# Four more transposes moved from TensorE to the DMA queue, and five instead of two put ahead of the loads of v

## The chip, the cores and the metric

One core of a Trainium2 chip. The time is the device time of one execution in microseconds (us); medians are over several executions.

## The reference

A block of 2048 rows of 512 numbers: a layer norm; attention over 8 dilated positions (32 heads of 16, the positions 0, 2, ... 14 rows back); a gated GELU network of width 1792 on the same normalized rows; the two multiplied and added to the input.

```python
xn = _layernorm(x, axis=-1)
s = _A_ref(xn, A_wqkv, A_wo)      # q, k, v = xn @ wqkv; softmax over 8 dilated positions; @ wo
g = _silu(_B_ref(xn, B_w_gate, B_w_up, B_w_down))   # (gelu(xn@w_gate) * (xn@w_up)) @ w_down
return x + s * g
```

## The kernel before

The rows are worked on in four chunks of 512 rows (`j`), each of four tiles of 128 (`t`). A chunk goes through the gated projections (`glu`, 14 pairs), the q, k, v projections of the *next* chunk (`qkv`), four down projections (`down`), and after the first of these through `sums`: the softmax's denominators, the sums over v, and the logits of the next chunk.

Projections read the normalized rows transposed (`xnT`). Tiles are transposed in one of two ways:

```python
    def to_psum(t, cs=range(NC)):                # on TensorE, into PSUM; ScalarE copies it out
        ...
            nc.tensor.transpose(
                trs[t][:, c * P : (c + 1) * P], xns[t][:, c * P : (c + 1) * P], ident[:]
            )

    def transpose_by_dma(t, cs=range(NC)):       # by the DMA, four of 128x128 a tile
        ...
        for c in cs:
            nc.sync.dma_start(
                out=xnT[j][:, c, i * P : (i + 1) * P],
                in_=xns[t][:, c * P : (c + 1) * P],
                transpose=True,
            )
```

In chunk 1, tiles 4 and 5 go over TensorE and tiles 6 and 7 over the DMA. All DMAs are issued from one queue, in program order. v takes a way through DRAM: `copy_out` stores it (`vT<-vst`), and `load_v` reads it back in four loads, shifted by the dilated positions (`v_arr<-vT`). In the stretch of interest the order is:

```python
    at(("glu", 0, 0), transpose_by_dma, TPQ + 2, (0, 1))     # tile 6, two of four
    at(("glu", 0, 0), load_v, 0)
    at(("glu", 0, 0), transpose_by_dma, TPQ + 2, (2, 3))
    at(("glu", 0, 0), transpose_by_dma, TPQ + 3)             # tile 7
    at(("glu", 0, 0), load_late_weights)                     # w_down, wo
```

VectorE takes from there: eight products with v (`pv`, line 409), then sixteen products of q and k for chunk 1 (`pk`, line 337), which TensorE sums to the logits:

```python
    def sums(j):
        if j + 1 < NJ:
            nc.scalar.preload_act_table(AF.Exp)
        denominators(j)
        av_sums(j)
        if j + 1 < NJ:
            logits(j + 1)
        reciprocals(j)
        ...
```

The softmax here doesn't subtract the row's maximum and nothing guards it: scores larger than these inputs give would overflow.

## Time and profile before

| | kernel before |
|---|---|
| median of the first three runs | 228.55 us (228.47 to 228.56) |
| TensorE busy | 98% of the span |
| VectorE, ScalarE busy | 67%, 58% |
| first load of v issued, fourth landed | 26.11, 40.20 us |
| first product with v starts | 40.33 us |
| first gated projection to first output projection | 52.62 us |

The last row is the measure for what happens in the stretch concerned: from the start of the first `g_ps` matmul to that of the first `s_ps` matmul, read from the trace. The profile of the kernel before is of an execution of 228.39 us. The lines of the profile are in the prediction.

To read them: the span is the time from the first to the last instruction; the chain is the work that ended last, followed back step by step to what released it. PE is TensorE (PEld its weight loads), DVE is VectorE, ACT is ScalarE, POOL is GpSimd, SPq is the sequencer that issues the DMAs, and L311 is line 311 of the kernel. "x4" counts instructions, and a bracket gives the idle time before one and what ended it.

### The profile page before, as it was taken

To read this page: it belongs to the slowest core of one execution; us is meant where nothing else is said; L and a number is where in the kernel's file an instruction comes from. 1 tells how busy PE (TensorE), PEld (TensorE's weight loads), DVE (VectorE), ACT (ScalarE), POOL (GpSimd) and SP (SyncE) were. 2 spreads that over 40 slices of the span, in tenths; PEclk is the share of its full clock that TensorE was granted. 3 is DMA by queue.
4 is the path that set the end of the run, shared out by engine and by line. 5 is a ranking of instruction groups with operands and counts; after the bars stand their busy time and mean duration, and the time that the engine had idled before them with its cause. 6 is when DMAs were issued, how large, how long until landed. Compare 5 with 4: busy or idle time off the path is not lost.

```text
span 226.7 us, 3599 instructions
## 1 busy us (share of the span) xinstructions
PE 221.7 (98%) x1324; PEld 107.0 (47%) x1324; DVE 152.4 (67%) x280; ACT 132.1 (58%) x209; POOL 20.1 (9%) x67
## 2 busy tenths in 40 slices
PE   7999999999999999999999999999999999999993
PEld 4885444444444444444444444444444444444453
DVE  4689971999995489969813859925934448971434
ACT  4488679767631767676752466676763356756210
POOL 1026941000030000320000000000000000000000
PEclk9999999999999999999999999999999999999999
DMA  6999399942049921100219931100208940001002
GB/s 192 375 397 382 82 215 166 315 115 94 7 101 198 184 58 25 23 4 0 93 41 212 184 105 29 25 2 0 92 21 163 199 121 0 0 0 33 0 25 69
DMA packets 30130, 24.64 MB, mean 109 GB/s; under 512 B 10784, under 2 KB 29600, under 8 KB 30112
## 3 DMA queue, kind: packets, MB, share of 16 engines
q1 hardware_dynamic: 30112, 24.41, 45.0%
q8 instruction: 10, 0.16, 0.3%
q14 instruction: 8, 0.07, 0.1%
HBM read 18.74 MB, written 4.34 MB: 102 GB/s over the span
## 4 chain that ended last, share of the span: by engine, by line
PE 96%; DVE 1%; DMA 1%; issue 0%; ACT 0%; DVEq 0%
PE y_ps L460 21%; PE g_ps L266 21%; PE u_ps L266 21%; PE qkv_ps L266 16%; PE s_ps L476 6%; PE L_ps L355 3%; PE o_ps L423 3%; PE qk_ps L578 2%; DMA x_sb<-in_A_x_dram 1%; PE v_ps L578 1%; PE tr L224 1%; DVE stats L187 1%; PE den_ps L375 0%; DVE m L484 0%; DVE mv L190 0%
## 5 line engine op out<-in xcount | busy, mean ns | idle before, releaser
L266 PE MATMUL g_ps<-xnT,wg_sb 128*128 128x512 bf16 x224 | 57.5, 379 | 0.0
L266 PE MATMUL u_ps<-xnT,wu_sb 128*128 128x512 bf16 x224 | 57.5, 379 | 0.0
L460 PE MATMUL y_ps<-wd_sb,h 128*128 128x512 bf16 (+1 forms) x238 | 49.9, 367 | 0.0
L450 ACT ACTIVATE u<-u_ps 128x512 bf16<-128x512 f32 x56 | 33.5, 598 | 16.9 <-PE u_ps L266 16.9
L452 DVE TENSOR_TENSOR h<-ge,u 128x512 bf16<-128x512 bf16 x56 | 23.8, 424 | 29.0 <-ACT u L450 27.3
L448 ACT ACTIVATE ge<-g_ps 128x512 bf16<-128x512 f32 x56 | 33.5, 598 | 16.4 <-PE g_ps L266 16.3
L337 DVE TENSOR_TENSOR pk<-q_sb,k_sb 128x1024 bf16<-128x1024 bf16 (+1 forms) x56 | 38.9, 759 | 4.6 <-ACT k_sb L290 4.6
L409 DVE TENSOR_TENSOR pv<-E,v_arr 128x1024 bf16<-128x1024 bf16 (+1 forms) x48 | 39.7, 862 | 0.0
L266 PE MATMUL qkv_ps<-xnT,wqkv_sb 128*128 128x512 bf16 (+1 forms) x192 | 37.0, 352 | 0.0
L460 PEld LDWEIGHTS <-h 128*128 128x128 bf16 x238 | 23.0, 98 | 25.9 <-issue 1.3
L266 PEld LDWEIGHTS <-wu_sb 128*128 128x128 bf16 x224 | 21.9, 98 | 26.4
L266 PEld LDWEIGHTS <-wg_sb 128*128 128x128 bf16 x224 | 21.7, 98 | 26.3 <-issue 0.8
L468 ACT ACTIVATE sl<-y_ps 128x512 bf16<-128x512 f32 (+1 forms) x17 | 9.7, 572 | 32.6 <-PE y_ps L460 32.6
L266 PEld LDWEIGHTS <-wqkv_sb 128*128 128x128 bf16 x192 | 18.8, 98 | 17.6
L484 DVE TENSOR_TENSOR m<-s_ps,sl 128x512 bf16<-128x512 f32 (+1 forms) x17 | 11.1, 655 | 19.1 <-PE s_ps L476 19.1
L435 DVE TENSOR_TENSOR oT<-o_ps,rb 128x1024 bf16<-128x1024 f32 x8 | 9.4, 1219 | 11.7 <-DMA rb<-rs_d 11.7
L476 PE MATMUL s_ps<-wo_sb,oT 128*128 128x512 bf16 (+1 forms) x68 | 14.8, 366 | 0.0
L204 POOL TENSOR_TENSOR rstd<-rstd,mhalf 128x1 f32<-128x1 f32 x12 | 8.0, 670 | 71.1 <-DVE rstd L201 71.1
L290 ACT ACTIVATE vst<-qkv_ps 128x512 bf16<-128x512 f32 x14 | 8.4, 597 | 3.7 <-PE qkv_ps L266 3.7
L290 ACT ACTIVATE k_sb<-qkv_ps 128x512 bf16<-128x512 f32 x14 | 8.4, 602 | 3.2 <-PE qkv_ps L266 3.2
L290 ACT ACTIVATE q_sb<-qkv_ps 128x512 bf16<-128x512 f32 x14 | 8.3, 603 | 3.0 <-PE qkv_ps L266 3.0
L476 PEld LDWEIGHTS <-oT 128*128 128x128 bf16 x68 | 6.6, 98 | 7.2
(58 smaller groups left out, 126.6 us busy)
## 6 DMA issues: line engine op xcount, KB each, us to landing
v_arr<-vT SPq DMA_DIRECT2D x16, 520.0 KB, 8.4
vT<-vst SPq DMA_DIRECT2D x8, 256.0 KB, 2.3
out_dram<-o_t SPq DMA_DIRECT2D x15, 128.0 KB, 2.7
wg_sb<-in_B_w_gate_dram SPq DMA_DIRECT2D x2, 896.0 KB, 10.0
wu_sb<-in_B_w_up_dram SPq DMA_DIRECT2D x2, 896.0 KB, 10.7
wd_sb<-in_B_w_down_dram SPq DMA_DIRECT2D x1, 1792.0 KB, 10.8
wqkv_sb<-in_A_wqkv_dram SPq DMA_DIRECT2D x4, 384.0 KB, 4.6
x_sb<-in_A_x_dram SPq DMA_DIRECT2D x3, 512.0 KB, 10.3
```

The costliest lines, as they stand in the source:

```text
L266: nc.tensor.matmul(ps, lhsT=w[:, dk, lo : lo + P], rhs=xnT[j][:, dk, i0 : i0 + n], start=(dk == 0), stop=(dk == NC - 1),)
L290: nc.scalar.activation(out=dst, in_=ps, func=AF.Copy)
L337: nc.vector.tensor_tensor(out=st[j]["pk"][w][:, c0 : c0 + n, :], in0=st[j]["q"][:, c0 : c0 + n, :], in1=k_sb[j][:, c0 : c0 + n, off : off ...
L409: nc.vector.tensor_tensor(out=pv[:, d : d + n, :], in0=st[j]["E"][:, wh, :].unsqueeze(1).to_broadcast([P, n, TQ]), in1=st[j]["va"][:, 4 * ...
L435: nc.vector.tensor_tensor(out=oT[:, g : g + 2, :], in0=st[j]["o"][:, g : g + 2, :], in1=st[j]["rb"][:].unsqueeze(1).to_broadcast([P, 2, TQ ...
L448: nc.scalar.activation(out=ge[:], in_=g_ps[:], func=AF.Gelu_apprx_tanh)
L450: nc.scalar.activation(out=u[:], in_=u_ps[:], func=AF.Copy)
L452: nc.vector.tensor_tensor(out=h[:], in0=ge[:], in1=u[:], op=ALU.mult)
L460: nc.tensor.matmul(y[:], lhsT=st[j][fc][:, tt * P : (tt + 1) * P], rhs=wd_sb[:, fc, cols], start=(fc == 0), stop=(fc == NF - 1),)
L468: nc.scalar.activation(out=sl[:], in_=y[:], func=AF.Silu)
L476: nc.tensor.matmul(s[:], lhsT=st[j]["oT"][:, g, tt * P : (tt + 1) * P], rhs=wo_sb[:, g, cols], start=(g == 0), stop=(g == NC - 1),)
L484: nc.vector.tensor_tensor(out=m[:], in0=s[:], in1=sl[:], op=ALU.mult)
```

## The change

TensorE is the bound, so four transposes of tile 5 are taken from it. The queue stands idle for 3.8 us ahead of the loads of v, so three transposes are put into that hole: five stand ahead of the loads instead of two, seven behind instead of six.

```diff
     for i in range(TPQ):
         at(("down", 0, 1), moments, 2 * TPQ + i)
-        if i < 2:
-            at(("glu", 0, i), transpose, TPQ + i)
         at(("down", 0, 2), normalize, 2 * TPQ + i)
...
-    at(("glu", 0, 0), transpose_by_dma, TPQ + 2, (0, 1))
+    at(("glu", 0, 0), transpose, TPQ)
+    at(("glu", 0, 0), transpose_by_dma, TPQ + 1)
+    at(("glu", 0, 0), transpose_by_dma, TPQ + 2, (0,))
     at(("glu", 0, 0), load_v, 0)
-    at(("glu", 0, 0), transpose_by_dma, TPQ + 2, (2, 3))
+    at(("glu", 0, 0), transpose_by_dma, TPQ + 2, (1, 2, 3))
     at(("glu", 0, 0), transpose_by_dma, TPQ + 3)
```

## The prediction

> **What bounds the kernel now.** I read the page's busy shares and chain first, then the chain between 16 and 22 us, where the removed transposes stand, then the DMA issues and landings, and last VectorE's timeline to the place where its work meets TensorE again.
>
> ```profile
> PE 221.7 (98%) x1324; PEld 107.0 (47%) x1324; DVE 152.4 (67%) x280; ACT 132.1 (58%) x209; POOL 20.1 (9%) x67
> ...
> PE 96%; DVE 1%; DMA 1%; issue 0%; ACT 0%; DVEq 0%
> ```
>
> TensorE is busy for 98% of the span and makes up 96% of the chain that ended last. What leaves its instruction stream shortens the run, unless another engine or a transfer then makes it wait.
>
> ```profile
> 18.46 0.86 PE u_ps L266 x4
> 19.33 0.22 PE tr L224 x4
> 19.55 0.86 PE g_ps L266 x4
> ```
>
> This is the chain (start, length, what). The four transposes of tile 5 stand on it as 0.22 us between two projections; no wait surrounds them.
>
> The DMA queue of the kernel before (start, length of the issuing):
>
> ```profile
> 17.16 2.30 SPq L295 DMA_DIRECT2D vT<-vst  x2
> 19.55 2.75 SPq L258 DMA_TRANSPOSE xnT<-xn  x2
> 26.11 2.67 SPq L311 DMA_DIRECT2D v_arr<-vT  x4
> 28.83 7.70 SPq L258 DMA_TRANSPOSE xnT<-xn  x6
> 36.79 0.40 SPq L116 DMA_DIRECT2D wd_sb<-in_B_w_down_dram  x1
> ...
> SPq L311 <- DMA vT<-vst: 3.7, 1, 3.7
> ```
>
> After two transposes the queue stands from 22.30 to 26.11, because the loads of v wait until the stores of v to DRAM have landed (issued at 18.04, landed 8.0 us later). Three transposes fit into this hole: the change is made to use it. The last line is from the queue's own waits.
>
> VectorE's timeline:
>
> ```profile
> 39.87 0.42 DVE L452 TENSOR_TENSOR h<-ge,u 128x512 bf16<-128x512 bf16 x1 [0.56 <-ACT u L450]
> 40.33 1.23 DVE L409 TENSOR_TENSOR pv<-E,v_arr 128x2048 bf16<-128x2048 bf16 x1
> ...
> 44.67 0.42 DVE L452 TENSOR_TENSOR h<-ge,u 128x512 bf16<-128x512 bf16 x1 [0.17 <-ACT u L450]
> 45.01 5.76 DVE L409 TENSOR_TENSOR pv<-E,v_arr 128x2048 bf16<-128x2048 bf16 x5
> 50.69 9.71 DVE L337 TENSOR_TENSOR pk<-q_sb,k_sb 128x1024 bf16<-128x1024 bf16 x16
> ```
>
> The fourth load of v was issued at 28.16 and took 12.0 us, so it landed at 40.20. The first product that reads v starts at 40.33, 0.04 us after VectorE became free. So this landing is just on time, and only just. From there VectorE has no idle time until 60.40, the end of the last q-k product, but for 0.17 us at 44.67 and two hundredths elsewhere.
>
> The logits' matmuls, in the chain, in the stretch after the gated projections of chunks 0, 1 and 2 (a chunk is 512 rows, four tiles):
>
> ```profile
> 59.28 1.77 PE L_ps L355 x32
> ...
> 113.18 1.73 PE L_ps L355 x32
> ...
> 167.04 1.73 PE L_ps L355 x32
> ```
>
> The same 32 matmuls take 0.04 to 0.05 us longer at 59.28. In the trace the matmul of the last product starts at 60.456, which is 0.054 after that product's end at 60.402, while its three neighbours started at 60.40. So TensorE already waits there, about 0.05 us, for VectorE. This is the place that decides the change.
>
> **What the Trainium skill says.** "VectorE: DVE Perf Modes", section The three transpose paths, gives 390 ns for a 128x128 bf16 transpose on TensorE and 1309 ns by the DMA crossbar. The trace shows 219 ns for one on TensorE, but four of them follow each other by 0.056 us, so only 0.22 us for four stand on the path; one DMA transpose holds the issuing queue for 1.23 us and, with nothing else in flight (at 88 us), lands 2.3 us after its issue. "DMA: Bandwidth & Descriptors", section Queues, rings and completion order, says that on each DMA engine descriptors are consumed in ring order. The trace agrees: the transposes issued behind the loads of v land only after the last of these (the last one, issued at 35.30, after 6.9 us, at 42.2). The same page, section Anatomy of one DMA, says that a wait is made by the issuing sequencer before it dispatches. The trace agrees with the 3.7 us above.
>
> **The change part by part.** (1) TensorE loses 4 transposes: 4 x 0.056 = 0.22 us, all on the path. (2) ScalarE loses one copy out of PSUM, 0.59 us at 19.86; it waits for TensorE just after, so nothing on the path. A PSUM buffer comes free earlier; TensorE does not wait for one there. (3) Three more transposes stand ahead of the loads of v. Steps from issue to issue are 1.54 for the first (19.55 to 21.09) and 1.27 for the others: the five start at 19.55, 21.09, 22.36, 23.64, 24.91 and the loads at 26.18, against 26.11. That is +0.07 us. The stores of v may also land a little later beside these transposes, and the first packets of v come about 1.3 us after their issue, close behind the fifth transpose: I allow +0.08 for both. (4) Seven instead of six transposes stand behind. They do overlap the tail of the loads, since DMA engines which finished their share of v go on to them. From the issue of the first load of v to the landing of the fourth, the kernel before takes 13.27 us in chunk 3 (nothing transposed behind), 13.52 and 14.01 in chunks 2 and 1 (four behind) and 14.09 in chunk 0 (six behind). That is 0.1 to 0.14 per transpose: +0.1. Sum of (3) and (4): v lands 0.25 us later, at about 40.45.
>
> (5) Eight landing semaphores are used in turn, as the program's list of waits shows. With four more DMAs the down weights now wait for the fourth load of v: issued at 40.5 instead of 36.8. They took 10.8 us, most of it behind v, and landed at 47.6; I expect about 49, needed at 54.1 by the first y. No cost. The eleventh transpose waits for the third load of v (landed 36.8), still ahead of the fourth's landing. The last transpose should land at 42.21 + 0.22 + 0.25 = 42.7, and the next projections, which read it, start at 43.78 - 0.22 = 43.56. No cost, with 0.9 us to spare.
>
> **The sum on VectorE's side.** Call the later landing of v d. The first v product starts at 40.33 + d, since TensorE's lead cannot help it. The products up to 44.50 follow without idle time. There the 0.17 us of waiting for ScalarE goes away, as ScalarE is 0.22 earlier with TensorE. So the last q-k product ends at 60.40 + d - 0.17, and TensorE, coming 0.22 earlier, must wait for it. The net change is d - 0.17, at best -0.22 from the transposes alone. With d = 0.25: +0.08 us. From 228.55 this makes 228.63, so 228.6. The gain on TensorE is given back at the logits of chunk 1, as a wait for VectorE of some 0.3 us.
>
> **The rivals.** *Everything is gained.* v lands no later, or the products have slack that I do not see: -0.17 to -0.22, 228.35. For it: the hole of 3.8 us takes three transposes of 1.27 nearly exactly, and the stores' landing, not the queue, released the loads. Against it: the product starts within 0.13 us of v's landing. *The loads of v are clearly later.* Where the three transposes hold up the stores' last packets, or the loads' first ones, d could be 0.5 to 1.0: 228.9 to 229.4. For it: the crossbar's packets around 38 us took 72 to 86 ns each, and only about 16 where they ran alone around 64 us, so transposes and loads do disturb each other; against: the DMA engines are nearly idle from 24 to 27.4 us (a busy share of 0.09, then 0.03 and 0.00). *The transposes become the wait.* If the seven behind land after 43.6, the projections of chunk 1 stand still; this needs 0.9 us more than estimated, and would make 229 or more. For it: these are all of tile 7 and most of tile 6, the projections read them in their first four matmuls. Against: the six before landed at 0.2 to 0.5 us intervals after v, and the down weights will not be in their way any more.
>
> **Range and chances.** The best that the change can do is 228.3. The central case is 228.6, the two bad rivals reach 229.4; I give them a fifth together, and cut the range at 229.2. A change of 2% is 4.6 us; nothing here has that size except a transfer landing 5 us late, so faster 0.01, same 0.97, slower 0.02.
>
> **What would show it.** TensorE: 1320 matmuls, ScalarE: 208 instructions, the chain without the second row of four transposes; projections from 19.33 on 0.22 earlier. Queue: loads of v issued at 26.1 to 26.3, five transposes from 19.55. The fourth load of v lands at 40.3 to 40.7; the down weights are issued only then. The first v product starts right after it and the wait of 0.17 at 44.67 is gone. The logits at 59 take 1.9 to 2.1 us in the chain instead of 1.77. If the logits still take 1.77 and v is no later, I am wrong and the gain is whole; if TensorE waits at 43.6, the third rival holds.

## The result, and the profile after

The changed kernel took 229.16 us (median of 6; 228.67 to 229.88), the kernel before in the same rounds 228.56 us (228.47 to 228.84). The ratio is 1.0026 (95% interval 1.0008 to 1.0044): 0.6 us slower, and spread over 1.2 us instead of 0.4. A ratio here is the mean of one kernel's fast runs over the mean of the other's in the same rounds, so not quite the ratio of the medians.

The page and the chain of the kernel after:

```profile
PE 222.2 (98%) x1320; PEld 106.9 (47%) x1320; DVE 152.1 (67%) x280; ACT 131.7 (58%) x208; POOL 19.9 (9%) x67
...
PE 80%; DVE 10%; DMA 6%; SPq 1%; issue 1%; ACT 0%; DVEq 0%; ACTq 0%
```

Four matmuls and one copy of ScalarE are gone. But of the chain, 10% are now VectorE's and 6% DMA; before, 96% were TensorE's. In order of time, the chain first shows the gain (start, length, what):

```profile
18.47 0.86 PE u_ps L266 x4
19.33 0.86 PE g_ps L266 x4
```

The projection starts at 19.33 instead of 19.55. From here on TensorE is 0.22 us earlier. The DMA queue of the kernel after (start, length of the issuing):

```profile
17.16 2.52 SPq L295 DMA_DIRECT2D vT<-vst  x2
19.77 6.73 SPq L258 DMA_TRANSPOSE xnT<-xn  x5
26.61 2.71 SPq L311 DMA_DIRECT2D v_arr<-vT  x4
```

The five transposes start 0.22 us later than the two did (the second store's issue took that much longer in this execution), take 6.73 us and leave no hole. The loads of v follow at once, at 26.61. The queue's own waits of this profile no longer have a row for these loads; before, they had waited 3.7 us for the stores. The stores landed at 25.64 here, so the loads could have left 0.9 us sooner. VectorE's timeline, and the chain between 28 and 62 us (DVEq and SPq are the sequencers of VectorE and of the queue):

```profile
40.98 1.23 DVE L409 TENSOR_TENSOR pv<-E,v_arr 128x2048 bf16<-128x2048 bf16 x1 [0.91 <-DMA v_arr<-vT]
...
45.06 0.42 DVE L452 TENSOR_TENSOR h<-ge,u 128x512 bf16<-128x512 bf16 x1
```

```profile
28.67 12.08 DMA v_arr<-vT
40.75 0.03 issue
40.77 0.05 DVEq L409
40.82 0.06 issue
40.88 0.05 DVEq L409
40.93 0.04 issue
40.98 1.23 DVE pv L409
...
51.16 9.64 DVE pk L337 x16
60.80 0.04 issue
60.84 0.59 PE L_ps L355 x5
61.44 0.75 PE y_ps L460 x3
```

The first product with v starts 0.65 us later than before and VectorE waited 0.91 us for it. The 0.17 us of idle time at the fourth `h` are gone. The last q-k product ends at 60.79 instead of 60.40, and the last five logits' matmuls stand behind it: the chain goes over from VectorE to TensorE exactly there. From first to last, the 32 logits' matmuls start over 2.18 us; before, over 1.57. The next down projection starts at 61.44 instead of 61.05, so the 0.22 us are gone and 0.39 us with them. The span agrees: 227.0 against 226.7 us.

This execution took 228.67 us. It was the fastest of the six, so 0.3 of the 0.6 us have been found and the slower executions remain to be explained.

### The profile page after: what moved, and what is told of

Its sections match the earlier page's. It is cut to its first block, busy times and chain, and to the rows that moved or that the text cites. A ratio compares the mean times of both kernels' runs of the same rounds, so it can differ in the third digit from the quotient of the medians.

```text
span 227.0 us, 3597 instructions
## 1 busy us (share of the span) xinstructions
PE 222.2 (98%) x1320; PEld 106.9 (47%) x1320; DVE 152.1 (67%) x280; ACT 131.7 (58%) x208; POOL 19.9 (9%) x67
## 4 chain that ended last, share of the span: by engine, by line
PE 80%; DVE 10%; DMA 6%; SPq 1%; issue 1%; ACT 0%; DVEq 0%; ACTq 0%
PE y_ps L460 20%; PE g_ps L266 18%; PE u_ps L266 18%; PE qkv_ps L266 11%; PE s_ps L476 6%; DMA v_arr<-vT 5%; DVE pk L337 4%; DVE pv L409 3%; PE o_ps L423 2%; PE L_ps L355 2%; PE qk_ps L576 2%; DMA x_sb<-in_A_x_dram 1%; SPq L311 1%; PE v_ps L576 1%; DVE h L452 1%
```

## The experiments

**Theory A**: five transposes outlast the landing of the stores of v, so the queue itself delays the loads of v; v is just on time, VectorE has nearly no slack from there to the logits of chunk 1, and TensorE waits there. **Rival B**: the transposes behind are too many or too late, and slow the loads down or keep the projections of chunk 1 waiting. **Rival C**: any transpose put ahead delays the stores' own packets.

Values of profiles, in us (one execution each; "stretch" is the measure defined above; "logits" is from the first to the last of the 32 matmuls' starts):

| kernel | ahead, behind | stores landed | first load issued | fourth landed | first product | logits | stretch |
|---|---|---|---|---|---|---|---|
| before | 2, 6 | 26.04 | 26.11 | 40.20 | 40.33 | 1.57 | 52.62 |
| after | 5, 7 | 25.64 | 26.61 | 40.75 | 40.98 | 2.18 | 53.00 |
| after_again | 5, 7 | 25.84 | 26.64 | 40.71 | 40.94 | 1.94 | 52.76 |
| after_third | 5, 7 | 26.39 | 28.25 | 42.41 | 42.64 | 2.87 | 54.16 |
| before_a5_b3 | 5, 3 | 26.08 | 27.31 | 41.41 | 41.64 | 2.18 | 53.23 |
| a6_b6 | 6, 6 | 26.10 | 27.96 | 41.97 | 42.09 | 2.90 | 53.73 |
| a4_b8 | 4, 8 | 25.62 | 25.69 | 40.24 | 40.42 | 1.60 | 52.43 |
| a4_b8_again | 4, 8 | 25.63 | 25.69 | 40.10 | 40.29 | 1.59 | 52.42 |
| a3_b9 | 3, 9 | 26.35 | 26.41 | 40.61 | 40.69 | 1.80 | 52.63 |
| a3_b9_again | 3, 9 | 26.20 | 26.26 | 40.57 | 40.65 | 1.71 | 52.54 |
| a2_b10 | 2, 10 | 26.47 | 26.54 | 40.66 | 40.78 | 1.52 | 53.30 |
| after_late | 5, 7 | 25.95 | 27.91 | 42.02 | 42.25 | 1.53 | 52.92 |
| before_late | 2, 6 | 26.45 | 26.52 | 40.92 | 41.04 | 1.53 | 52.80 |
| a4_b8_late | 4, 8 | 26.03 | 26.09 | 40.55 | 40.74 | 1.53 | 52.57 |

### The same kernel again: after_again

> The changed kernel once more, as the control of this batch and for a second profile. All theories expect 228.7 to 229.9 and a ratio to the kernel before of about 1.0026. Theory A (the loads of v leave the queue late because five transposes ahead outlast the stores' landing) expects in its trace: first load of v issued at 26.4 to 27.2, at least 0.5 us after the stores landed; first product of v released by the load of v, not by VectorE; a hole of TensorE at the logits of chunk 1 of 0.6 us or more. If this execution is slower than 228.67, A expects the load of v or that hole to be later by the same amount. Rival B (the seven transposes behind end too late) expects a hole of TensorE at 43.6 to 44.3 us, ahead of the projections of chunk 1.

No edit. Measured: 229.40 us median (228.66 to 229.81), ratio 1.0034 (1.0021 to 1.0046). The profile fell once more on the fastest execution, 228.66. The loads left 0.79 us after the stores had landed. The wait at the logits was smaller than A had expected (1.94 us of spread, 0.4 more than where nothing waits), and there was no hole ahead of the projections of chunk 1, as B had it. The time holds; the slow executions stay unseen.

### Four ahead, eight behind: a4_b8

```diff
     at(("glu", 0, 0), transpose_by_dma, TPQ + 1)
-    at(("glu", 0, 0), transpose_by_dma, TPQ + 2, (0,))
     at(("glu", 0, 0), load_v, 0)
-    at(("glu", 0, 0), transpose_by_dma, TPQ + 2, (1, 2, 3))
+    at(("glu", 0, 0), transpose_by_dma, TPQ + 2)
```

> Only tile 5's four transposes ahead of the loads of v, eight behind. Theory A: the first load is issued at 25.7 to 26.1, set free by the stores' landing again; its fourth lands at 39.8 to 40.3; the logits' wait is 0.2 us or less; time 228.3 to 228.6, ratio to before 0.999 to 1.000. Rival B: eight behind instead of seven make it worse: last transpose after 43.6 us, hole ahead of the projections of chunk 1, 229.3 or more. Rival C (any transpose added ahead holds the stores' own packets up): the stores land 0.2 us or more later than in the kernel before, and the time lies between, 228.8 to 229.0.

Measured: 228.84 us median (228.12 to 229.13), ratio 0.9999 (0.9984 to 1.0014). The queue's waits and its timeline:

```profile
SPq L311 <- DMA vT<-vst: 0.4, 1, 0.4
```

```profile
19.75 5.40 SPq L258 DMA_TRANSPOSE xnT<-xn  x4
25.69 2.73 SPq L311 DMA_DIRECT2D v_arr<-vT  x4
```

With one transpose fewer the stores' landing sets the loads free again (a wait of 0.4 us), and in this profile nearly the whole 0.22 us is kept: the stretch is 52.43 against 52.62. B expected this kernel to be worse than the changed one; it is better. C expected the stores to land later; they landed at 25.62. But half of the executions took 229 us, so that the median lies above A's 228.3 to 228.6 (the ratio is within its range), which A does not explain yet.

### The order alone: before_a5_b3

The kernel before, with tile 5 on TensorE as it was:

```diff
-    at(("glu", 0, 0), transpose_by_dma, TPQ + 2, (0, 1))
+    at(("glu", 0, 0), transpose_by_dma, TPQ + 2)
+    at(("glu", 0, 0), transpose_by_dma, TPQ + 3, (0,))
     at(("glu", 0, 0), load_v, 0)
-    at(("glu", 0, 0), transpose_by_dma, TPQ + 2, (2, 3))
-    at(("glu", 0, 0), transpose_by_dma, TPQ + 3)
+    at(("glu", 0, 0), transpose_by_dma, TPQ + 3, (1, 2, 3))
```

> The order alone: the kernel before (tile 5 on TensorE) with five of its eight transposes ahead of the loads of v and three behind. Theory A: first load at 26.5 to 26.8, fourth landing at 40.4 to 40.8, first product later by 0.2 to 0.6 us, and as TensorE gains nothing here the logits wait 0.2 to 0.5 us: time 228.6 to 229.2, ratio 1.000 to 1.003. Rival B: with three behind instead of six it is the same as before or faster, 228.3 to 228.6.

Measured: 229.44 us (228.84 to 230.88), ratio 1.0043 (1.0019 to 1.0066). So the order alone does the harm, and with only three transposes behind: this speaks against B. The loss is larger than A had expected. The timeline of the queue shows why:

```profile
23.48 2.45 SPq L258 DMA_TRANSPOSE xnT<-xn  x1
```

The fourth of the five transposes held the queue for 2.45 us instead of 1.23, and the first load of v left at 27.31. The trace has an instruction fetch of 8 KB over the DMA engines from 23.13 on, which took 1.76 us. In the kernel before such a fetch was as long (1.66 us from 23.4 on), but there the queue was in its hole and had nothing to issue.

### The logits moved out of the way: after_late

```diff
@@ sums(j)
-        if j + 1 < NJ:
+        if 0 < j and j + 1 < NJ:
             nc.scalar.preload_act_table(AF.Exp)
...
-        if j + 1 < NJ:
+        if 0 < j and j + 1 < NJ:
             logits(j + 1)
@@ the loop over down(j, tt)
+                if j == 0 and tt == 1:
+                    nc.scalar.preload_act_table(AF.Exp)
+                    logits(1)
```

> The changed kernel with the logits of chunk 1 computed after the second down projection instead of after the first, 3 us later on TensorE, so that a late VectorE costs nothing there. Theory A, with the loss passing only through the wait at these logits: v as late as in the changed kernel (fourth load landing at 40.5 or later), but no hole on TensorE and the whole 0.22 us gained: 228.2 to 228.5, ratio 0.998 to 1.000. Rival B (hole ahead of the projections of chunk 1): no better than the changed kernel, 229.0 to 229.3.

Measured: 228.70 us (228.44 to 229.65), ratio 1.0004 (0.9990 to 1.0019), on the same chip as after_again with 1.0034: 0.7 us better, but above the 228.2 to 228.5 that A had expected. The profile fell on an execution with v very late: the fourth load landed at 42.02, which is 1.8 us later than before. Still the logits were not spread (1.53 us). The kernel a6_b6 below had v at 41.97, its logits in the old place, and a stretch of 53.73; here it is 52.92. So the loss goes through the wait at the logits. Not all came back, though: the chain shows that TensorE did wait for transposes ahead of the projections of chunk 1, which is rival B's hole, here as a consequence of the late loads:

```profile
34.59 9.36 DMA xnT<-xn
43.95 0.14 issue
44.09 2.53 PE qkv_ps L266 x11
```

From the first gated projection to these projections it took 26.47 us, against 26.12 in the first profile of the changed kernel: 0.35 us. The stretch adds up: 52.62 of the kernel before, less 0.22 for the transposes, plus 0.35 here and 0.22 for the edit's own price (next section) is 52.97, measured 52.92.

### Late logits by themselves, and both cures: before_late, a4_b8_late

> The kernel before with only the logits of chunk 1 moved behind the second down projection. Theory A: it waits only 0.05 us there, so at most 0.05 us is gained: ratio 0.999 to 1.0005. A gain of 0.3 us or more would say that unprofiled executions of the kernel before also lose time at the logits, which A does not expect. A loss of 0.2 us or more would say that moving the logits costs something of its own.

> Both cures at once: four transposes ahead of the loads of v, eight behind, and the logits of chunk 1 after the second down projection. Theory A: neither the loads of v nor the logits hold TensorE back, so the whole 0.22 us of the removed transposes is gained: ratio to the kernel before 0.998 to 0.9995, about 228.2 to 228.5, and no hole of TensorE over 0.1 us from 20 to 62 us. If late logits cost something by themselves (a table load, a buffer), the ratio is 1.000 or more, and the same kernel with the old order of transposes (sent with it) shows it too.

The same edit on the kernel before gave 229.01 us (228.51 to 229.12), ratio 1.0009 (0.9997 to 1.0022); on the kernel with four ahead 228.62 us (228.39 to 228.74), ratio 0.9995 (0.9983 to 1.0008). The ratio of the first and the time of the second are above what I had expected (1.0005 and 228.5 us at most), and the chain of before_late shows a price of the edit:

```profile
59.71 3.13 PE y_ps L460 x14
62.84 1.84 PE L_ps L355 x32
```

The down projection takes 3.13 instead of 3.02 us and the logits 1.84 instead of 1.73: two more changes between 128-column and 32-column weights, and 0.11 us more at each. The kernel before shows the same around the logits of chunk 0, which stand between projections: 1.84 us, and 0.97 instead of 0.86 for the projection after them. So in these profiles late logits take the wait for a late v away, for 0.2 us. As the removed transposes bring 0.22, nothing is won together. TensorE had no wait between 20 and 62 us with both edits, as A had expected.

### The cost doubled: a6_b6

```diff
-    at(("glu", 0, 0), transpose_by_dma, TPQ + 2, (0,))
+    at(("glu", 0, 0), transpose_by_dma, TPQ + 2, (0, 1))
     at(("glu", 0, 0), load_v, 0)
-    at(("glu", 0, 0), transpose_by_dma, TPQ + 2, (1, 2, 3))
+    at(("glu", 0, 0), transpose_by_dma, TPQ + 2, (2, 3))
```

> The suspected cost doubled: six transposes ahead, six behind. Theory A: the first load is issued at 27.8 to 28.2 us (29 where a transpose's issue is held up), its fourth lands at 41.8 to 42.5, the logits wait 1.2 to 2 us; time 229.9 to 230.8, ratio 1.006 to 1.010. Rival B (the number behind matters): six behind instead of seven is no worse than the changed kernel, 228.8 to 229.2.

Measured: 230.27 us (229.80 to 230.73), ratio 1.0069 (1.0055 to 1.0084), both in A's range. Its chain:

```profile
30.01 11.96 DMA v_arr<-vT
41.97 0.03 issue
41.99 0.05 DVEq L409
42.04 0.04 issue
42.09 1.23 DVE pv L409
...
52.27 9.64 DVE pk L337 x16
61.91 0.04 issue
61.95 0.59 PE L_ps L355 x5
```

The load's issue, its landing, the products, the logits: each step of A, 1.1 to 1.35 us later than in the first profile of the changed kernel. Of this, 0.38 us is that this execution reached its first gated projection later; the stretch is 0.73 us longer, and the logits' spread grew by the same 0.73. The queue took more than one transpose's time in addition, since the fourth transpose held it for 1.82 us.

### Three ahead, nine behind: a3_b9, a3_b9_again, beside a4_b8_again

```diff
-    at(("glu", 0, 0), transpose_by_dma, TPQ + 1)
-    at(("glu", 0, 0), transpose_by_dma, TPQ + 2, (0,))
+    at(("glu", 0, 0), transpose_by_dma, TPQ + 1, (0, 1, 2))
     at(("glu", 0, 0), load_v, 0)
-    at(("glu", 0, 0), transpose_by_dma, TPQ + 2, (1, 2, 3))
+    at(("glu", 0, 0), transpose_by_dma, TPQ + 1, (3,))
+    at(("glu", 0, 0), transpose_by_dma, TPQ + 2)
```

> Three ahead, nine behind. Theory A: the loads leave when the stores have landed, 25.7 to 26.2, with 1.2 us to spare in the queue for a held-up transpose, so the fourth landing and the logits are as in the kernel before. But the eighth transpose behind waits for the fourth load's landing at about 40.2 (eight landing semaphores in turn), and the ninth follows 1.25 us later and lands at 43.9 to 44.2, needed by the fourth matmul of the projections at 44.2: time 228.3 to 228.7, ratio 0.999 to 1.001, hole of TensorE at 44 us of 0 to 0.3 us. Rival B in its strong form (each transpose behind costs) expects 229.3 or more.

> The best order so far once more, to see whether its gain holds on another chip. Theory A (loads leave with the stores' landing, spare time in the queue for one held-up transpose): ratio to the kernel before 0.998 to 1.000 and a spread of at most 0.4 us over its executions. If the gain of the first time was chance, the ratio lies at 1.000 or above.

> Four ahead once more, beside three ahead on one chip. Theory A with held-up transposes: four end at about 25.2 us, less than 1 us before the stores have landed, so an execution in which one of them is held up by 1.2 us loses part of it: ratio 0.999 to 1.001, spread larger than that of three ahead (0.6 us or more), mean at least 0.2 us above it. If held-up transposes don't matter, it is equal to three ahead.

Three ahead: 228.39 us (228.28 to 228.51), ratio 0.9987 (0.9973 to 1.0000); a second time 228.47 us (228.29 to 228.58), ratio 0.9990 (0.9978 to 1.0003). Four ahead on the chip of the second: 228.44 us in the median but 227.98 to 230.49, ratio 1.0013 (0.9980 to 1.0046). Both of my expectations on the spread held; the ratio of four ahead lies above the 0.999 to 1.001 that I had expected. The queue's waits of a3_b9:

```profile
SPq L311 <- DMA vT<-vst: 2.6, 1, 2.6
SPq L258 <- DMA v_arr<-vT: 2.2, 2, 1.5
```

The loads again wait for the stores, and 2.6 us of the hole are left, enough for a transpose that is held up. In both profiles of three ahead the long fetch was there (1.60 and 1.61 us), but the last of the three had been issued as it began. In both of four ahead the fetch was a short one, 0.37 us; so their profiles are of good executions, and what the execution of 230.49 us lost was not seen. In a4_b8_late, the one profile of four ahead with a long fetch, the held transpose ended at 25.87, just before the stores landed at 26.03, so it cost nothing there: that held-up transposes make the slow executions of four ahead is not shown.

The profiles of three ahead don't show the gain either. In both, v landed 0.4 us later than in the profile of the kernel before, the logits spread by 0.24 and 0.14 us more, and the stretch (52.63 and 52.54 against 52.62) gave most or all of the 0.22 us back. These executions took 228.39 and 228.38 us, the profiled one of the kernel before 228.39. The medians differ since most executions of the kernel before are slower than its profiled one, and what they lose was not seen.

### Two ahead, ten behind: a2_b10

```diff
-    at(("glu", 0, 0), transpose_by_dma, TPQ + 1)
-    at(("glu", 0, 0), transpose_by_dma, TPQ + 2, (0,))
+    at(("glu", 0, 0), transpose_by_dma, TPQ + 1, (0, 1))
     at(("glu", 0, 0), load_v, 0)
-    at(("glu", 0, 0), transpose_by_dma, TPQ + 2, (1, 2, 3))
+    at(("glu", 0, 0), transpose_by_dma, TPQ + 1, (2, 3))
+    at(("glu", 0, 0), transpose_by_dma, TPQ + 2)
     at(("glu", 0, 0), transpose_by_dma, TPQ + 3)
```

> Two ahead, ten behind: the other end of the same choice. Theory A: the loads of v leave as in the kernel before, but the eighth transpose behind waits for the fourth load (40.2 us), so the tenth is issued at 42.7 to 43.2 and lands at 45.0 to 45.6, while the fourth matmul of the projections wants it at 44.2: a hole of TensorE of 0.8 to 1.3 us there and none at the logits; time 229.0 to 229.7, ratio 1.002 to 1.005. If only what stands ahead of the loads counts, it is as good as three ahead: 0.998 to 1.000.

Measured: 229.35 us (229.19 to 229.69), ratio 1.0031 (1.0018 to 1.0043). The chain:

```profile
28.59 12.07 DMA v_arr<-vT
40.66 0.02 issue
40.67 1.18 SPq L258
41.85 0.04 issue
41.90 1.23 SPq L258
43.13 0.04 issue
43.17 2.33 DMA xnT<-xn
45.50 0.04 issue
45.55 9.87 PE qkv_ps L266 x45
```

Here rival B is the case: the eighth transpose behind waits for the landing of the fourth load, as eight landing semaphores are used in turn; two more follow, the last lands at 45.50, and TensorE waits for it with the fourth matmul of the projections. The hole is 0.95 us (those first four matmuls start over 1.60 instead of 0.65 us). The logits don't wait at all. So there is a bound on both sides, and three ahead lies between.

### A slow execution of the changed kernel: after_third

> The changed kernel a third time, for a profile of one of its slower executions: the two profiles so far fell on its fastest ones (228.66 and 228.67, while the others are 229.0 to 229.9). Theory A with a held-up transpose: if this execution takes 229.0 or more, its trace shows one of the five transposes held in the queue for 1.8 us or more beside a long instruction fetch near 23 us, the first load of v at 27.2 to 28, its fourth landing at 41.3 to 42, and the logits' matmuls spread over 2.5 us or more. If it is slow without these, the cause of the slower executions is another and stays open. If it is again 228.7, nothing new is learnt.

Measured: 230.33 us, one execution (state unknown; the kernel before beside it took 228.66, and the granted clock was 1.0). This is the execution that was wanted: the held-up transpose, the long fetch and the wide spread came as A had expected, the loads and their landing even later than its ranges (28 and 42 us at most). The queue, and then its third transpose alone:

```profile
19.71 8.43 SPq L258 DMA_TRANSPOSE xnT<-xn  x5
28.25 2.73 SPq L311 DMA_DIRECT2D v_arr<-vT  x4
```

```profile
22.54 3.05 SPq L258 DMA_TRANSPOSE xnT<-xn  x1
```

The instruction fetch, as a share of 16 DMA engines in the stretch from 22.9 to 25.4 us, first of this execution and then of the first profile of the changed kernel:

```profile
q14 instruction: 1, 0.01, 5.3%
```

```profile
q14 instruction: 1, 0.01, 0.9%
```

16 engines over 2.5 us are 40 us, so the fetch took 2.1 us here and 0.4 us there. The third transpose held the queue for 3.05 us, and the loads left 1.86 us after the stores' landing. The rest is the chain as before, later: v at 42.41, the last q-k product at 62.45. The stretch is 54.16, 1.16 us more than in the first profile; the start of this execution was slower by 0.5 us as well. TensorE also waited for transposes ahead of the projections: these start 26.59 us after the first gated projection, 0.47 us more than in the first profile (the profile's list of waits has 0.3 of it). With the 0.69 us by which the logits spread more, this is the whole 1.16. So slow executions of the changed kernel are of this kind at least in one case.

That the fetch holds the transpose up is a coincidence in time, not shown by taking it away. It is a close one. In all five profiles with a long fetch and a transpose held up, the transpose's issue ended at one of two distances behind the fetch's end: 0.39 us (after_third, a6_b6, after_late) or 1.03 us (before_a5_b3, a4_b8_late). And in all ten profiles with a long fetch, those without a held-up transpose too, the stores landed 1.01 us (two ahead) or 1.19 us (three or more) after its end. So the fetch may itself have waited beside the stores, and which of them sets the time is open. The lengths: in the nine profiles in which a transpose was issued between 23 and 26 us, the fetch and the longest transpose ahead of the loads (leaving out the first of them, which took 1.4 to 1.6 us everywhere) were 0.37 and at most 1.40 us (after, after_again, a4_b8, a4_b8_again), 1.28 and 1.82 (a6_b6), 1.29 and 2.35 (a4_b8_late), 1.76 and 2.45 (before_a5_b3), 1.78 and 2.66 (after_late), 2.13 and 3.05 (after_third). Why a fetch is sometimes long stays open.

## Why the prediction was right

The time, 229.16 us, lies within 228.3 to 229.2, near its upper end; the central value of 228.6 was too low. The mechanism is the predicted one: the gain on TensorE is given back at the logits of chunk 1, as a wait for VectorE. What was off is above all one term, the size of the delay of v (d): 0.54 us at the landing and 0.65 at the first product in the first profile, where the prediction had 0.25. So the sum came out as +0.39 us in the stretch instead of +0.08. That the time still fell into the range is partly luck: the control's median was 229.40.

- **TensorE's gain of 0.22 us.** As predicted: 19.33 instead of 19.55, kept up to the logits. ScalarE's copy cost nothing on the path.
- **The transposes ahead delay v by 0.15 us** (0.07 in the queue, 0.08 for packets). This is the term that was mis-sized. The loads left 0.50 us later than before in the first profile and 2.14 us later in the slow one (which had reached its first gated projection 0.51 us later). I had added up the shortest steps of the queue, 1.27 us each, and compared the sum with the landing of the stores in one execution. The steps came to 1.27 to 1.44 us in the two fast profiles, the stores landed up to 0.4 us earlier, so that 0.8 to 1.0 us were lost against them; and I had not asked what happens when one transpose is held up. The 3.8 us hole was the reserve for this, and the change used it up.
- **The transposes behind add 0.1 us.** Not confirmed. From the first load's issue to the fourth's landing it took 14.10 us with three behind, 14.01 to 14.40 with six, 14.07 to 14.16 with seven, 14.41 to 14.56 with eight, 14.20 to 14.31 with nine and 14.12 with ten: no trend. So the differences between chunks on which I had based it are not shown to come from this number; they were also less even than I had written (0.06 and 0.19 us per transpose in chunks 2 and 1, 0.14 in chunk 0).
- **The weights and the last transposes cost nothing.** The down weights were issued at 40.76 and landed at 49.96, in time for the y at 54. The last transpose landed at 43.43, later than the predicted 42.7, and still 0.8 us ahead of its matmul: it was this one, the twelfth and not the eleventh, that waited for the third load of v (landed at 37.60; the transpose was issued at 37.62). In the slow execution the last landed at 45.03 and TensorE did wait, 0.3 to 0.5 us: the third rival came true there.
- **VectorE's chain passes d - 0.17 us on.** Right in form. The first product came 0.65 us later, the last q-k product ended 0.39 later. The slack at the fourth `h` was 0.25 us rather than 0.17, because VectorE's instructions overlap by 0.08 us and the profile's idle time is counted from an end to a start. And d grew by 0.11 us behind the landing: VectorE's queue goes through the four loads' waits in two steps, and the fourth load's wait is in the first step in the changed kernel, so the second step comes after the landing (two rows of DVEq in the chain above; one in a6_b6).
- **The wait at the logits of 0.3 us**: seen, with 0.6 us in the first profile and 1.3 in the slow one (spreads of 2.18 and 2.87 us over the 1.57 of before).

The rival in which v is clearly later, with 228.9 to 229.4 us, was thus the nearest to what came, though for another reason than the one given: not the packets of transposes and loads disturbed each other, but the queue was full. (The packets of "around 64 us" that stood for it were not transposes: none was in flight from 42.2 to 67.3 us in the kernel before, where the reciprocals were stored and loaded.) B alone and C fell by a4_b8, before_a5_b3 and a6_b6. Against C speaks every profile: the second store landed 7.98 to 8.22 us after its issue with two or three transposes ahead and 7.57 to 7.85 with four to six, so sooner and not later. Why is open.

With three transposes ahead the kernel took 228.39 and 228.47 us, 0.1% less than the kernel before. This is the size of the removed 0.22 us, but one interval ends at 1.0000 and the other includes 1, and the two profiles give back most or all of the 0.22, so a gain over the kernel before is not shown. Against the changed kernel (229.16 and 229.40) it is clear: the intervals of the ratios, 0.9973 to 1.0003 and 1.0008 to 1.0046, lie apart.

## What to carry to other kernels

An idle stretch of a queue just ahead of a transfer that is just on time is not free room but a reserve: fill it only as far as the queue still waits for the transfer's own condition in every execution, and look at more than one profile, since the first may be of the best execution. To see whether a transfer is on time, compare its landing with the start of the first instruction that reads it, and then follow that engine to the next place where the bounding engine needs it.

## What the Trainium skill lacked or had wrong

- "Runtime: NRT & Kernel Launch", section Instruction fetch mechanics, calls the fetch "mostly hidden". Here the profile has an 8 KB instruction fetch near 23 us that took 0.37 us in four executions and 1.28 to 2.20 us in ten; in five of these ten a DMA transpose was held in the issuing queue beside it, for 1.82 to 3.05 us instead of 1.23. That the fetch is the cause is not shown.
- "VectorE: DVE Perf Modes", section The three transpose paths, gives one time for each path. What counted here were others: 0.056 us from one to the next in TensorE's stream, 1.23 us of the issuing queue for a DMA transpose of 128x128, and 2.3 us from its issue to its landing where nothing else was in flight, up to 12 us behind loads.
- "TensorEngine Tiling (Array Packing)" has no figure for what a change of the tiling costs. Here 0.11 us came with each change between 128-column and 32-column weights.
- No page gives what a wait for several DMA semaphores costs VectorE after the last landing: 0.08 to 0.12 us from landing to start where one waiting step was left, 0.18 to 0.23 us where two were.
